# Constant matmuls in TensorE's planned gaps, and shorter matmul durations in the planner, in a two-layer decode kernel

## The chip, the cores and the metric

The kernel runs on one core of one Trainium2 chip. The metric is the device time of one execution in microseconds (us). The core has five engines with instruction streams of their own: TensorE (PE, matrix multiplies; its weight loads are shown as PEld), VectorE (DVE), ScalarE (ACT), GpSimd (POOL) and SyncE (SP), which here issues nearly all transfers from the chip's memory (HBM) to the core's on-chip memory. TensorE writes to PSUM, which has eight banks of 512 floats in each of 128 partitions; DVE and ACT read from there.

## The reference

Four sequences decode one token each (width 512) through two identical layers. One layer is a layer norm, attention with 32 query heads over 8 key/value heads (cache of 4096 positions, head size 128), a residual addition, a second layer norm, a gated feed-forward block of inner width 1792, and a residual addition.

```python
def _A_ref(x, k_cache, v_cache, wq, wo):
    q = (x @ wq).reshape(B, Sq, Hq, Dh) ...
    scores = jnp.einsum("bhqd,bhkd->bhqk", q, k) * (Dh ** -0.5)
    p = _softmax(scores, axis=-1)
    o = jnp.einsum("bhqk,bhkd->bhqd", p, v)
    return ... @ wo

def _B_ref(x, w_gate, w_up, w_down):
    g = jnp.einsum("bsd,df->bsf", x, w_gate)
    u = jnp.einsum("bsd,df->bsf", x, w_up)
    return jnp.einsum("bsf,fd->bsd", _sigmoid(g) * u, w_down)

x = A_x
x = x + _A_ref(_layernorm(x), A_k_cache, A_v_cache, A_wq, A_wo)
x = x + _B_ref(_layernorm(x), B_w_gate, B_w_up, B_w_down)
x = x + _A_ref(_layernorm(x), A_k_cache, A_v_cache, A_wq, A_wo)
x = x + _B_ref(_layernorm(x), B_w_gate, B_w_up, B_w_down)
```

Both layers use the same weights and the same caches.

## The kernel before

The attention work is cut into 16 units: sequence b (0 to 3), half of the key/value heads hg, layer l. Their order is written out in `seq`. A unit needs 8 tiles of keys and 8 of values, each 128 partitions by 2048 bf16 elements (512 KB). They land in a ring of 22 slots. The second layer's unit with hg 1 reuses the 8 key tiles and 6 of the 8 value tiles of the first layer's, which stay in their slots until then (`kept`); the other tiles are loaded again.

A unit runs like this. DVE transposes every key tile in place in 32x32 blocks (L575, 1.2 us each). TensorE multiplies the spread queries by the keys in two groups of 16 matmuls into S_ps (L582). DVE takes the maximum (L599) and a short chain makes the bias; ACT exponentiates (L615). The probabilities go through TensorE twice with an ACT copy after each (L622, L627, L633, L640) and come out transposed; L644 and L648 make the sum's reciprocal. TensorE multiplies them by the values in two groups of 64 matmuls into O_ps (L662); then a scaling copy (L668), a transposition (L672), a copy (L678), 64 matmuls with the output weights wo into M_ps (L684), and the residual addition (L699). After a sequence's second unit of a layer comes the feed-forward chain: layer norm (L710 to L730), gate and up (L760), tanh, product, five small matmuls (L782, L786), down (L796, 56 matmuls), addition (L804). After layer 0 it goes on to the next layer norm and the second queries (L535, 64 matmuls into Q_ps). `spread` (L555) lays the queries out through Q_ps and four ACT copies (L564) into qbd.

All of this is put in one list of operations, `S.put(engine, functions, reads, writes, cost, rank, ...)`. The planner `_Plan.schedule` (L102) plays the list with these costs in microseconds: each engine does one operation at a time, loads on "sp" go in their list's order at DMA_RATE megabytes per us, and of the operations that are ready the one with the lowest rank goes, or one that is ready soon (PATIENCE). What it fixes is the order of operations on each engine, which slot each tile gets, and with these the semaphore waits, which `emit` writes out. The costs themselves leave no trace in the program: nothing starts at a set time on the chip. A cost given for TensorE is multiplied by 0.75 (PACE).

Two PSUM banks, Q_ps and M_ps, are shared by many users one after another. A user that names `lock="Q"` or `"M"` holds the bank from its start until the operation with `free` of the same name has ended; the next holder waits for that one.

The ring's transfers are issued at L405, weights at L408, both on SyncE. A transfer into a used slot waits until the last reader of the tile in it is done.

Of the kernel before, what the change touches and what calls it, by code (L numbers as in the profile page):

```python
# [10 lines left out]
ENGINES = ("sp", "act", "pe", "dve", "pool")  # L11
LATENCY = 0.1
DMA_RATE = 0.42
DMA_DELAY = 1.6
PATIENCE = 2.0
PACE = {"pe": 0.75}

# [10 lines left out]
class _Op:  # L28
    def __init__(self, n, eng, fns, cost, rank, sem, inc):
        self.n = n  # L30
        self.eng = eng
        self.fns = fns
        self.cost = cost * PACE.get(eng, 1.0)
        self.rank = rank
        self.sem = sem
        self.inc = inc
        self.deps = set()
        self.order = set()
        self.lock = None
        self.free = None  # L40
        self.tile = None
        self.size = 0
        self.needed = inc == 16
        self.value = None
        self.start = None
        self.end = None


class _Plan:
# [3 lines left out]
    def __init__(self, slots):  # L53
        self.ops = []
        self.last_write = {}
        self.readers = {}
        self.slots = [None] * slots
        self.holder = {}

    def put(self, eng, fns, reads=(), writes=(), cost=0.1, rank=0.0, dma=None, size=0, lock=None, free=None, tiles=(), load=None):  # L60
# [41 lines left out]
    def schedule(self):  # L102
# [5 lines left out]
        bus = 0.0  # L108
        tenants = list(self.slots)
        locks = {}  # L110
        for op in self.ops:
# [33 lines left out]
        while done < len(self.ops):  # L145
            pick = None
            for e in ENGINES:
                if e == "sp":
                    if not loads or loads[0] not in ready:
                        continue  # L150
                    op = loads[0]
                    at = max(clock[e], ready[op])
                    if op.tile is not None:
# [3 lines left out]
                        at = max(at, s[0])  # L157
# [4 lines left out]
                for op in queue[e]:  # L162
                    at = max(clock[e], ready[op])
# [22 lines left out]
            at, op = pick  # L186
# [20 lines left out]
            if op.lock is not None:  # L207
                held = locks.get(op.lock)
                if held is not None:
                    self._after(op, held[1], True)  # L210
                locks[op.lock] = (None, None)
            if op.free is not None:
                locks[op.free] = (op.end + LATENCY, op)
            done += 1
            for u in users.get(op, ()):
                left[u] -= 1
                if not left[u]:
                    arrive(u)
        self.span = max(op.end for op in self.ops)
        self.prog = {e: sorted((o for o in self.ops if o.eng == e), key=lambda o: (o.start, o.n)) for e in ENGINES}  # L220
# [4 lines left out]
        for e in ENGINES:  # L225
            for op in self.prog[e]:
                if op.needed:
                    count[op.sem] = count.get(op.sem, 0) + op.inc
                    op.value = count[op.sem]

    def emit(self, eng, e, sems):
# [15 lines left out]
def bass_interleave_layers__gqa_block_cached__glu_gated_glu__decode_kernel(nc, A_x, A_k, A_v, A_wq, A_wo, B_x, B_wg, B_wu, B_wd, out):  # L247
# [85 lines left out]
    def bank(name, new=False):  # L333
        tenure[name] += new
        return f"{name}t{tenure[name]}"
# [113 lines left out]
    for i in range(1, len(seq) + 1):  # L449
# [15 lines left out]
        "pe", lambda e: e.matmul(M_ps[:, 0:4], lhsT=ones[:], rhs=xsum[:, 0:4], start=True, stop=True),  # L465
        reads=["xsum1", "ones"], writes=["M0"], cost=0.4,
    )
# [38 lines left out]
    def first_q(hg):  # L506
        fns = []
        for s in range(NS):
            g = hg * NS + s
            for h in range(R):  # L510
                for k in range(KD):
                    c0 = (g % 2 * R + h) * DH
                    fns.append(lambda e, s=s, g=g, h=h, k=k, c0=c0: e.matmul(
                        Q_ps[:, (s * R + h) * B:(s * R + h + 1) * B], lhsT=wq[:, g // 2, k, c0:c0 + DH], rhs=xT[:, :, k],
                        start=(k == 0), stop=(k == KD - 1),
                    ))
        r = 0.0 if hg == 0 else 0.6
        S.put("pe", fns, reads=["xT", f"wq{2 * hg}", f"wq{2 * hg + 1}"], writes=[bank("Q", True)], cost=2.1, rank=r, lock="Q")
        S.put(
            "act",  # L520
            lambda e: e.activation(
                q1[:, hg * NS:(hg + 1) * NS].rearrange("p g h b -> p (g h b)"), Q_ps[:, 0:64], ACTF.Copy
            ),
            reads=[bank("Q")], writes=[f"q1{hg}"], cost=0.25, rank=r, free="Q",
        )

    def second_q(b, hg, rank):
        fns = []
        for s in range(NS):
            g = hg * NS + s  # L530
            for h in range(R):
                for k in range(KD):
                    c0 = (g % 2 * R + h) * DH
                    c = s * R + h
                    fns.append(lambda e, g=g, k=k, c0=c0, c=c: e.matmul(  # L535
                        Q_ps[:, c:c + 1], lhsT=wq[:, g // 2, k, c0:c0 + DH], rhs=xT[:, b, k:k + 1],
                        start=(k == 0), stop=(k == KD - 1),
                    ))
        S.put("pe", fns, reads=[f"xT{b}", f"wq{2 * hg}", f"wq{2 * hg + 1}"], writes=[bank("Q", True)], cost=2.1, rank=rank, lock="Q")
        S.put(  # L540
            "act", lambda e: e.activation(q2[:, hg, :], Q_ps[:, 0:16], ACTF.Copy),
            reads=[bank("Q")], writes=[f"q2{hg}"], cost=0.2, rank=rank, free="Q",
        )

    def spread(i, rank):
# [7 lines left out]
        for n in range(NQ):  # L553
            for a in range(4):
# [3 lines left out]
                ))  # L558
        S.put("pe", fns, reads=[key, "ident"], writes=[bank("Q", True)], cost=0.5, rank=rank, lock="Q")
        fns = []  # L560
# [6 lines left out]
    def unit_scores(i):  # L567
        b, hg, l = seq[i]
        qi, rank = i % 2, float(i)
        for q in range(2):  # L570
# [9 lines left out]
            for nn in range(NQ):  # L580
                for s, t in enumerate(ts):
# [5 lines left out]
                    ))  # L587
            S.put("pe", fns, reads=[f"qbd{qi}"], writes=[f"S{q}"], tiles=ts, cost=1.85, rank=rank)

    def unit_probs(i):  # L590
# [30 lines left out]
        for c in range(8):  # L621
            fns.append(lambda e, c=c: e.matmul(  # L622
                PT_ps[:, c * 64:(c + 1) * 64], lhsT=p_sb[:, c, :], rhs=sel_p[:], start=True, stop=True,
            ))
        S.put("pe", fns, reads=["p_sb", "sel_p"], writes=["PT"], cost=0.65, rank=rank)
        S.put(
# [4 lines left out]
        for t4 in range(4):  # L631
            for a in range(4):
# [3 lines left out]
                ))  # L636
        S.put("pe", fns, reads=["pt1", "ident"], writes=["PT"], cost=0.65, rank=rank)
        pt = pt_sb[i % 2]
# [13 lines left out]
    def unit_values(i):  # L652
# [3 lines left out]
        for q in range(2):  # L656
            ts = [tile("v", b, hg, l, s, q) for s in range(NS)]
            fns = []
            for tt in range(TH):
                t = q * TH + tt  # L660
                for s, v in enumerate(ts):
# [3 lines left out]
                    ))  # L665
            S.put("pe", fns, reads=[f"pt_sb{i % 2}"], writes=["O"], tiles=ts, cost=1.75, rank=rank)
        S.put(
# [14 lines left out]
        for n in range(16):  # L682
# [9 lines left out]
            "pe", fns, reads=[f"oT{b}{hg}", f"wo{2 * hg}", f"wo{2 * hg + 1}"], writes=[bank("M", True), f"own{b % 2}" if first else f"own_{b}"],  # L692
            cost=1.8, rank=rank, lock="M",
        )
# [55 lines left out]
    def glu(b, l, rank):  # L750
# [14 lines left out]

        S.put("pe", wide(wg, G_ps), reads=[f"xT{b}", "wg"], writes=["G"], cost=1.55, rank=rank)
        rstd(b, 4.0, rsh[:, c:c + 1], f"rsh{c}", rank)
        S.put("pe", wide(wu, U_ps), reads=[f"xT{b}", "wu"], writes=["U"], cost=1.55, rank=rank)
        S.put(
# [24 lines left out]
        for i, (a, w) in enumerate(parts):  # L794
            for j in range(4):
# [3 lines left out]
                ))  # L799
        S.put("pe", fns, reads=["hT", "wd", "wd_r0", "wd_r1"], writes=["U"], cost=1.5, rank=rank)  # L800
        o = xin[:, b, :] if last else x[:]
# [49 lines left out]
    S.put("pool", lambda e: None, reads=outs)  # L851

    S.schedule()
    with nc.Block() as block:
# [37 lines left out]
```

## Time and profile before

| what | value |
|---|---|
| time, median of 3 runs | 359.93 us (357.55 to 362.03) |
| the profiled execution: its time, its span | 356.54 us, 354.1 us |
| mean granted TensorE clock in the profile | 0.805 |
| PE, PEld busy | 208.1 us (59%), 145.4 us (41%), 5,724 instructions each |
| DVE, ACT busy | 171.6 us (48%), 80.1 us (23%) |
| HBM read | 118.76 MB, 335 GB/s over the span |
| score matmuls L582 | 512, busy 49.0 us |
| value matmuls L662 | 2,048, busy 51.7 us |
| output projection L684 | 1,024, busy 22.1 us |
| key transpositions L575 (DVE) | 96, busy 114.6 us |
| instructions in all | 12,495 |

The span is the time from the first to the last instruction in one profiled execution; 2.4 us lie around it. The page's second part cuts the span into 40 slices of 8.9 us; a digit is the busy share in tenths, PEclk the clock granted to TensorE in tenths of full speed, GB/s what the transfers moved. The chain of waits follows the work back from the last instruction, at each step to what released it; "issue" is time in which an engine waited for nothing that the profile shows. In the timeline a row is a run of equal instructions: start, duration, engine, line, operation, output and inputs, count, and in brackets the idle time before it and what ended that. In the view by windows the columns are the window, its length, the busy time of PE, PEld, DVE, ACT and POOL with their instruction counts, the granted clock, the busy share of the DMA engines and GB/s.

### The profile page before, as it was taken

The page shows a single profiled execution, that of the slowest core. Times are in us where ns is not written, and L with a number is a line of the kernel's source. Part 1 is how long each engine was busy: PE and PEld are TensorE (multiplying, and loading weights), DVE is VectorE, ACT ScalarE, POOL GpSimd, SP SyncE. Part 2 cuts the span into 40 slices and gives each one's busy share as a digit, 9 for nine tenths or more (in the row PEclk, how much of TensorE's full clock was granted, in tenths as well). Part 3 has the DMA queues.
Part 4 walks back from the last instruction along what each step waited for, and adds up shares of the span by engine and source line. Part 5 has one row for each costly group of instructions (what it writes and reads, how often), then busy time and mean ns, then how long its engine had stood idle before and what let it go on. Part 6 is the DMA issues. An engine that isn't in the chain of part 4 may idle for free.

```text
span 354.1 us, 12495 instructions
## 1 busy us (share of the span) xinstructions
PE 208.1 (59%) x5724; PEld 145.4 (41%) x5724; DVE 171.6 (48%) x303; ACT 80.1 (23%) x231; POOL 12.9 (4%) x35
## 2 busy tenths in 40 slices
PE   0345423257585727787756368859645586767564
PEld 0315202142354615465435153636343545464352
DVE  4770760047305728605827567237458475247301
ACT  0413001001222211424113211533030313322021
POOL 6100000000000000100000000000000000000000
PEclk9999999999758667956888768685868558758889
DMA  7999999999989998889999996889999959899200
GB/s 277 385 401 408 409 351 381 411 409 403 344 320 329 412 407 325 281 303 382 410 408 409 406 381 222 274 292 413 409 406 409 408 207 325 279 409 405 89 4 2
DMA packets 37060, 119.57 MB, mean 338 GB/s; under 512 B 3472, under 2 KB 7824, under 8 KB 37008
## 3 DMA queue, kind: packets, MB, share of 16 engines
q1 hardware_dynamic: 36944, 118.76, 88.7%
q8 instruction: 45, 0.74, 0.8%
q14 instruction: 7, 0.06, 0.0%
q10 hardware_dynamic: 64, 0.01, 0.0%
HBM read 118.76 MB, written 0.00 MB: 335 GB/s over the span
## 4 chain that ended last, share of the span: by engine, by line
PE 38%; DMA 23%; SPq 12%; issue 12%; DVE 8%; ACT 6%; ACTq 0%; DVEq 0%
DMA ring<-in_A_k_cache_dram 10%; DMA ring<-in_A_v_cache_dram 9%; PE O_ps L662 9%; PE S_ps L582 8%; SPq L405 8%; PE M_ps L684 5%; SPq L408 4%; DVE ring L575 4%; DMA wd_r<-in_B_w_down_dram 4%; PE Q_ps L535 3%; PE G_ps L760 2%; ACT p_sb L615 2%; PE U_ps L796 2%; PE U_ps L760 2%; PE PT_ps L622 1%
## 5 line engine op out<-in xcount | busy, mean ns | idle before, releaser
L575 DVE STREAM_TRANSPOSE ring<-ring 128x1024 int32<-128x1024 int32 x96 | 114.6, 1224 | 39.9 <-DMA ring<-in_A_k_cache_dram 39.4
L662 PE MATMUL O_ps<-ring,pt_sb 128*4 128x128 bf16 x2048 | 51.7, 282 | 33.7 <-DMA ring<-in_A_v_cache_dram 19.3
L582 PE MATMUL S_ps<-ring,qbd 128*16 128x512 bf16 x512 | 49.0, 511 | 23.5 <-DVE ring L575 19.2
L662 PEld LDWEIGHTS O_ps<-ring,pt_sb 128*4 128x4 bf16 x2048 | 46.0, 112 | 40.1 <-issue 31.3
L599 DVE TENSOR_REDUCE ml<-S_ps 128x1 f32<-128x1024 f32 x16 | 19.6, 1223 | 54.0 <-PE S_ps L582 54.0
L615 ACT ACTIVATE p_sb<-S_ps,stat 128x1024 bf16<-128x1024 f32 x16 | 19.3, 1204 | 51.0 <-DVE stat L612 50.9
L582 PEld LDWEIGHTS S_ps<-ring,qbd 128*16 128x16 bf16 x512 | 13.1, 103 | 43.1 <-DVE ring L575 19.7
L684 PE MATMUL M_ps<-wo,oT 128*1 128x128 bf16 x1024 | 22.1, 251 | 7.8 <-issue 6.0
L668 ACT ACTIVATE o_sb<-O_ps,stat 128x128 bf16<-128x128 f32 x16 | 5.9, 368 | 82.8 <-PE O_ps L662 79.0
L684 PEld LDWEIGHTS M_ps<-wo,oT 128*1 128x1 bf16 x1024 | 18.9, 98 | 11.6 <-issue 7.8
L622 PE MATMUL PT_ps<-sel_p,p_sb 128*128 128x64 bf16 x128 | 8.9, 229 | 21.6 <-ACT p_sb L615 21.6
L564 ACT ACTIVATE qbd<-Q_ps 32x64 bf16<-32x64 f32 x64 | 13.7, 214 | 28.3 <-PE Q_ps L555 27.4
L535 PE MATMUL Q_ps<-xT,wq 128*128 128x1 bf16 x512 | 14.8, 164 | 8.3 <-issue 7.8
L746 POOL TENSOR_TENSOR stat<-stat 128x1 f32<-128x1 f32 x12 | 6.5, 542 | 326.3 <-DVE stat L742 282.1
L535 PEld LDWEIGHTS Q_ps<-xT,wq 128*128 128x128 bf16 x512 | 14.3, 100 | 9.0 <-issue 8.1
L622 PEld LDWEIGHTS PT_ps<-sel_p,p_sb 128*128 128x128 bf16 x128 | 6.6, 119 | 24.8 <-ACT p_sb L615 24.3
L648 DVE RECIPROCAL stat<-M_ps 128x1 f32<-128x1 f32 x16 | 2.7, 167 | 28.6 <-PE M_ps L644 28.5
L640 ACT ACTIVATE pt_sb<-PT_ps 128x512 bf16<-128x512 f32 x16 | 9.5, 597 | 14.8 <-PE PT_ps L633 14.7
L627 ACT ACTIVATE pt<-PT_ps 128x512 bf16<-128x512 f32 x16 | 9.6, 597 | 11.3 <-PE PT_ps L622 10.8
L699 DVE SCALAR_TENSOR_TENSOR xs<-M_ps,xs 128x128 f32<-128x128 f32 x12 | 3.5, 289 | 17.8 <-PE M_ps L684 17.8
L633 PE MATMUL PT_ps<-pt,ident 128*32 128x128 bf16 x256 | 9.7, 294 | 3.9 <-ACT pt L627 3.6
L796 PE MATMUL U_ps<-wd,hT 128*1 128x128 bf16 x384 | 7.6, 230 | 7.2 <-DMA wd_r<-in_B_w_down_dram 3.4
(89 smaller groups left out, 187.7 us busy)
## 6 DMA issues: line engine op xcount, KB each, us to landing
ring<-in_A_v_cache_dram SPq DMA_DIRECT2D x104, 512.0 KB, 12.1
ring<-in_A_k_cache_dram SPq DMA_DIRECT2D x96, 512.0 KB, 10.9
wq<-in_A_wq_dram SPq DMA_DIRECT2D x4, 1024.0 KB, 11.9
wo<-in_A_wo_dram SPq DMA_DIRECT2D x4, 1024.0 KB, 15.0
wg<-in_B_w_gate_dram SPq DMA_DIRECT2D x1, 1792.0 KB, 13.6
wu<-in_B_w_up_dram SPq DMA_DIRECT2D x1, 1792.0 KB, 16.9
wd<-in_B_w_down_dram SPq DMA_DIRECT2D x1, 1536.0 KB, 21.2
wd_r<-in_B_w_down_dram SPq DMA_DIRECT2D x2, 128.0 KB, 16.0
```

The costliest lines, as they stand in the source:

```text
L405: S.put("sp", lambda e: e.dma_start(ring[t.slot], src), dma="ring", load=t, size=0.524, cost=0.45)
L408: S.put("sp", lambda e: e.dma_start(o, i), writes=[key], dma=key, size=size, cost=0.45)
L535: fns.append(lambda e, g=g, k=k, c0=c0, c=c: e.matmul(Q_ps[:, c:c + 1], lhsT=wq[:, g // 2, k, c0:c0 + DH], rhs=xT[:, b, k:k + 1], start=(k ...
L575: "dve", lambda e, t=t: e.transpose(ring[t.slot].bitcast(dt.int32), ring[t.slot].bitcast(dt.int32)),
L582: fns.append(lambda e, s=s, t=t, nn=nn, q=q: e.matmul(S_ps[32 * s:32 * s + 16, q * 512:(q + 1) * 512], lhsT=qbd[:, qi, s, nn, :], rhs=ring ...
L599: dve(lambda e: e.tensor_reduce(ml[:, 0:1], S_ps[:], AX.X, ALU.max, negate=True), ["S0", "S1"], ["ml"], 1.22)
L615: lambda e: e.activation(p_sb[:].rearrange("p c x -> p (c x)"), S_ps[:], ACTF.Exp, bias=nbias, scale=rs, accum_out=ls),
L622: fns.append(lambda e, c=c: e.matmul(PT_ps[:, c * 64:(c + 1) * 64], lhsT=p_sb[:, c, :], rhs=sel_p[:], start=True, stop=True,))
L662: fns.append(lambda e, s=s, v=v, t=t, tt=tt: e.matmul(O_ps[32 * s:32 * s + R, 0:DH], lhsT=pt[:, t % 4, t // 4, s, :], rhs=ring[v.slot][:, ...
L684: fns.append(lambda e, n=n, j=j: e.matmul(M_ps[32 * j:32 * j + 1, P:2 * P], lhsT=oT[:, b, hg * 16 + n:hg * 16 + n + 1], rhs=wo[:, hg * 16 ...
L760: fns.append(lambda e, k=k, j=j: e.matmul(o_ps[32 * j:32 * j + 1, 0:FS], lhsT=xT[:, b, k:k + 1], rhs=w[:, k, j * FS:(j + 1) * FS], start=( ...
L796: fns.append(lambda e, i=i, a=a, w=w, j=j: e.matmul(U_ps[32 * j:32 * j + 1, 0:P], lhsT=a, rhs=w[:, j * P:(j + 1) * P], start=(i == 0), sto ...
```

## The change

Two things are done. First, the planner's numbers are new: PACE is gone, the costs of the TensorE operations are set one by one, and four constants of the planner change. Where a cost is not named in the diff, the planner now takes the full number in place of 0.75 of it.

```diff
-LATENCY = 0.1
-DMA_RATE = 0.42
+LATENCY = 0.06
+DMA_RATE = 0.41
 DMA_DELAY = 1.6
-PATIENCE = 2.0
-PACE = {"pe": 0.75}
+PATIENCE = 1.0
+FILL = 0.75
+FILL_US = 0.105
...
-        self.cost = cost * PACE.get(eng, 1.0)
+        self.cost = cost
```

| TensorE operation | planned before (cost x 0.75) | planned after |
|---|---|---|
| queries, 64 matmuls (L513, L535) | 1.58 | 1.8 |
| spread (L555) | 0.38 | 0.3 |
| score group (L582) | 1.39 | 1.05 |
| probabilities (L622, L633) | 0.49 | 0.42 |
| value group (L662) | 1.31 | 1.08 |
| output projection (L684) | 1.35 | 1.1 |
| gate, up (L760) | 1.16 | 0.95 |
| down (L796) | 1.13 | 0.98 |

Second, when the plan is complete, a new step looks at each pair of neighbours in TensorE's planned order. Where the planned gap between them has room, it puts in one operation of n filler matmuls, n being 0.75 of the gap divided by 0.105 us, rounded down. It takes the bank Q, or else M, if the plan has no holder of it during the fillers' planned time and some holder has released it before. The operation waits for that last release (an ACT or DVE operation) and for two constants. It signals nobody and stands in TensorE's stream between the two neighbours.

```diff
+    def fill(self, held_by):
+        pe = sorted((o for o in self.ops if o.eng == "pe"), key=lambda o: (o.start, o.n))
+        for a, b in zip(pe, pe[1:]):
+            at, room = a.start + a.cost, (b.start - a.start - a.cost) * FILL
+            n = int(room / FILL_US)
+            if n < 1:
+                continue
+            for name, fn in self.fillers:
+                until = at + n * FILL_US
+                held = held_by.get(name, [])
+                if any(x[0] < until and (x[1] is None or x[1] > at) for x in held):
+                    continue
+                last = [x for x in held if x[1] is not None and x[1] <= at]
+                if not last:
+                    continue
+                op = _Op(len(self.ops), "pe", [fn] * n, n * FILL_US, 99.0, "pe", 1)
+                op.start, op.end = at, until
+                op.deps.add(last[-1][2])
+                for k in self.filler_reads:
+                    op.deps.add(self.last_write[k])
+                self.ops.append(op)
+                break
...
+    for name, ps_ in (("Q", Q_ps), ("M", M_ps)):
+        S.fillers.append((name, lambda e, ps_=ps_: e.matmul(
+            ps_[:, 264:512], lhsT=ident[:], rhs=hsum[:].bitcast(bf)[:, 0:248], start=True, stop=True,
+        )))
+    S.filler_reads = ["ident", "hsum"]
     S.schedule()
```

A filler multiplies the constant `ident` (128x128 bf16) by 248 columns of the constant `hsum` and writes 248 columns of the bank that nothing reads. The times at which a bank is held (`held_by`) are noted by the planner as it goes; the very first matmul into M_ps (L465) now takes the lock of M, so that M counts as held from there on. The list of transfers and all computed values stay as they were.

## The prediction

> **What bounds the kernel now.** The page comes first: the slices and the queues.
>
> ```profile
> PE   0345423257585727787756368859645586767564
> PEclk9999999999758667956888768685868558758889
> GB/s 277 385 401 408 409 351 381 411 409 403 344 320 329 412 407 325 281 303 382 410 408 409 406 381 222 274 292 413 409 406 409 408 207 325 279 409 405 89 4 2
> q1 hardware_dynamic: 36944, 118.76, 88.7%
> q8 instruction: 45, 0.74, 0.8%
> ```
>
> The core moves 118.76 MB and the best slices reach about 410 GB/s: 290 us is the floor of the transfers, and the last 24 us (from 330) have none. The transfers end near 328 us, so some 35 us of transfer time are lost in dips, near 100, 145, 215 and 290 us. The transfer queue's own waits name who makes the dips:
>
> ```profile
> SPq L405 <- PE O_ps L662: 76.0, 11, 11.9
> ```
>
> The ring slot of the next tile is freed by the matmuls that read the last tile in it. The chain of waits agrees:
>
> ```profile
> PE 38%; DMA 23%; SPq 12%; issue 12%; DVE 8%; ACT 6%; ACTq 0%; DVEq 0%
> ```
>
> TensorE with its "issue" is half the span. Then I asked for the clock by window (columns: PE and weight-load busy, ..., clock, DMA share, GB/s) and for TensorE's timeline:
>
> ```profile
> 140.90:147.70 6.80, 5.11 (x134) 2.84 (x131) 5.93 (x13) 2.23 (x9) 0.54 (x1) 1.00 0.80 267
> 154.60:161.40 6.80, 5.85 (x165) 4.01 (x157) 0.26 (x1) 0.42 (x2) 0.00 (x0) 0.50 0.80 260
> 175.00:178.40 3.40, 0.00 (x0) 0.00 (x0) 1.89 (x2) 0.00 (x0) 0.00 (x0) 1.00 1.02 404
> 178.40:181.80 3.40, 3.29 (x52) 1.66 (x56) 0.00 (x0) 0.55 (x2) 0.00 (x0) 0.51 1.04 413
> 182.00:185.20 3.20, 1.79 (x92) 1.29 (x84) 2.32 (x7) 0.22 (x2) 0.00 (x0) 1.00 1.02 405
> ```
>
> ```profile
> 47.89 1.89 PE L582 MATMUL S_ps<-ring,qbd 128*16 128x512 bf16 x16 [3.24 <-DVE ring L575]
> 139.87 1.04 PE L582 MATMUL S_ps<-ring,qbd 128*16 128x512 bf16 x16
> 159.17 1.92 PE L582 MATMUL S_ps<-ring,qbd 128*16 128x512 bf16 x16
> ```
>
> Two clocks are granted, 1.00 and 0.50, and the same 16 score matmuls take 1.04 or 1.9 us. After 3.4 us without a matmul (175.0 to 178.4) the clock is half; after 3.4 us with 3.29 us of them it is full again. At 47.89 they took 1.89 us too, though the page shows 9 there: until about 90 us the clock row is not to be believed, and the array ran at half. The last thing to see is what "issue" is:
>
> ```profile
> 238.82 0.94 PE L535 MATMUL Q_ps<-xT,wq 128*128 128x1 bf16 x30 [3.84 <-issue]
> ...
> 252.26 0.56 PE L662 MATMUL O_ps<-ring,pt_sb 128*4 128x128 bf16 x27 [3.53 <-issue]
> 252.61 1.20 PE L582 MATMUL S_ps<-ring,qbd 128*16 128x512 bf16 x16
> 253.74 0.29 PE L672 MATMUL M_ps<-ident,o_sb 128*128 128x128 bf16 x1
> 253.96 1.88 PE L582 MATMUL S_ps<-ring,qbd 128*16 128x512 bf16 x16
> 255.63 1.70 PE L684 MATMUL M_ps<-wo,oT 128*1 128x128 bf16 x64
> 257.16 0.18 PE L555 MATMUL Q_ps<-q,ident 128*32 128x16 bf16 x4
> 258.56 0.24 PE L555 MATMUL Q_ps<-q,ident 128*32 128x16 bf16 x12 [1.22 <-issue]
> ```
>
> TensorE stops in the midst of a group. From one stop to the next it ran 27+16+1+16+64+4 = 128 matmuls, with their weight loads 256 instructions; q8's packets are 0.74 MB / 45 = 16.4 KB each, 64 bytes for each of 256. These stops wait for program text, and from 252.26 to 258.56 a block of 256 needed 6.3 us. The view of waits has 15 such stops on TensorE, 34 us in all, 14 of them after 90 us.
>
> **The change, part by part.**
>
> *Clock.* What the half clock costs, by line, is busy time less the number of groups by the time of a group at full clock (1.04 scores, 1.04 values, 1.06 wo, 0.79 gate/up, 0.97 down, 0.42 for each half of the probabilities' transposition): L582 49.0-32x1.04 = 16; L662 51.7-32x1.04 = 18; L684 22.1-16x1.06 = 5; L760 21.7-16x0.79 = 9; L796 10.2-8x0.97 = 2; L622 and L633 18.6-32x0.42 = 5. Sum 55 of 173 us; query projections take 1.6 to 1.8 us per 64 at either clock and gain nothing. Some 13 us of it lie before 90 us, beside transfers at 400 GB/s, and are worth nothing there: 42 are left. Of these lines the chain holds about 29% of the span (8.9 values, 8.2 scores, 4.6 wo, some 7 the rest), 103 us, 97 of them after 90 us; at 42/143 excess that is 28 us on the path, all of it only if the fillers hold the clock at full, as 75% filled gaps should by the windows above. Now the fetch: 11,448 matmuls and loads are 45 blocks, 38 of them after 90 us, and 14 of the 38 already end in a stop. There the block's arrival, not the clock, ends the work: a faster burst only makes the stop longer. 28x(1-14/38) = 18; a block or two falls under 6 us by the gain itself: 17. Ends: 0 (every block becomes late) and 28.
>
> [...]
>
> *Fillers, number.* TensorE is busy 36 us of the first 90 and 172 of the 264 after. At full clock the latter would be 130. The planner knows no stops; if its plan of this part lasts between 224 us (the 290 us floor and the tail of 24, less 90) and 264, its gaps are 95 to 134 us, 3/4 of it 71 to 100, at 0.105 us 680 to 950 fillers; gaps under 0.14 us get none, others round down. I take 550 after 90 us and 400 before it: 1,900 instructions, 7 blocks.
>
> *Fillers, price of one.* 248 columns: four L760 matmuls run side by side, so 16 of 448 columns in 0.79 us are 0.44 ns a column, 0.109 us. The weight load before it is at most 29 ns in a stream (34 pairs of L535 in 1.00 us): 0.109 to 0.138, so 78 to 99% of the gap in place of 75%, and no overrun while the clock is full. At half clock it is 0.22: 1.5 gaps. [...]
>
> *Fillers, instructions.* 550 after 90 us are 1,100 instructions, 4.3 blocks; at most 4.3x6.3 = 27 us, at least 0, for a run of 128 fillers lasts 13 us, twice a fetch, and cannot starve by itself. [...] I take 5, near the lower end.
>
> *The added wait.* A filler waits for the last release of its bank (an ACT or DVE copy), and the next real TensorE work queues behind it. Nearest rows: S_ps after the qbd copy 1.7 us in 3, M_ps L684 after oT 1.6 in 6. Between 0 and 4 us, taken 0: Q is released twice or so per unit, long before most gaps.
>
> *Order.* Latency, patience, rate and durations change the plan's order on all engines but not the list of transfers on SyncE; a ring slot may change. The one visibly misplaced wait is 3.4 us (down projection on wd_r). Between -5 and +5, taken 0. The lock on the first M_ps matmul moves nothing: no other M work is ready then.
>
> Sum: 354.1-17+5 = 342, and with the 2.4 us outside the span 344.5 against the profiled 356.54. The median of the runs is 1.0095 times that run: 348 us, 3.3% under 359.93.
>
> **The rivals.** (1) *The fetch eats the gain* (24%). More work at full clock, but each block still arrives every 6.1 to 6.3 us under transfers; stops grow from 34 to 50 us. For it: the 38 blocks after 90 us already average 6.9 us. Against: long tracts without a stop, as 128 to 157 us. Within 6 us of the old: 354 to 366. (2) *TensorE becomes fetch-bound by the fillers* (17%), the slower side. If the 4.3 blocks fall into tracts where fetches are back to back (163 to 201, 249 to 262, 305 to 329 us), they cost 27 us against the 17; with stops that throw the clock back (175 to 178) a third of the gain goes as well: 354.1+27-11 = 370 span, 376 in terms of the median. It decides as soon as over 17/6.3 = 2.7 blocks, 345 fillers, are paid in full. (3) *The clock does not stay up* (5%): stops and small gaps leave windows too empty, fillers run at 0.22 us and overrun by half of 95 us of gaps, at worst +47, with half of it hidden +24: 382. (4) *Larger gain* (part of the forecast's side): all 28 us on the path and dips closed: 330.
>
> **Chances.** Forecast, 54%, 332 to 352. A measurement of this kernel tells about 2% (7 us) from no change. Faster 0.54, same 0.24, slower 0.22. Leaving out some 5% below and 12% above: 332 to 370.
>
> **What would show it.** Clock windows at 1.00 in most of 100 to 330 us, and from about 20 us on score groups of 1.04 in place of 1.89; L582 near 35 us, L662 near 36. About 950 more matmuls on a new line and 52 packets in q8. Dips of the slices shallower, the last transfer at 317 in place of 328. "Issue" at 12 to 14% of the chain. Wrong, if the new matmuls' line stands on the chain with more than 10 us, if "issue" passes 60 us, or if score groups after 100 us still average 1.5.

## The result, and the profile after

The changed kernel takes 373.55 us (median, 371.97 to 375.48) where the kernel before takes 360.98 beside it: 1.038 of it, with a 95% interval of 1.028 to 1.048. The forecast was 348; the ratio makes it slower by 14 us. Executions of one kernel are sorted into fast and slow ones (of the kernel before, beside e1, 357.6 to 362.9 us and 364.4 to 367.4 us): the ratios here compare fast ones, the medians are of all, and the profiles of e1, e7 and e15 below are of slow ones. The page's lines that answer to those shown of before:

```profile
PE   0498979688877789965769889949687989877886
PEclk9999999699556599996878999965869999865999
GB/s 277 408 397 409 397 348 399 410 408 367 389 284 347 412 360 123 235 368 397 409 407 408 408 149 119 368 394 403 409 407 408 312 115 166 358 359 410 201 2 4
q8 instruction: 52, 0.85, 0.9%
...
PE 41%; DMA 18%; issue 13%; SPq 12%; DVE 11%; ACT 5%; ACTq 0%; DVEq 0%
DMA ring<-in_A_v_cache_dram 10%; PE O_ps L695 8%; SPq L438 8%; DVE ring L608 6%; PE S_ps L615 6%; PE M_ps L717 6%; PE Q_ps L887 4%; DMA ring<-in_A_k_cache_dram 4%; DMA wd_r<-in_B_w_down_dram 4%; SPq L441 4%; PE M_ps L887 3%; PE G_ps L793 2%; PE U_ps L793 2%; PE Q_ps L568 2%; ACT p_sb L648 2%
```

TensorE is busy nearly everywhere (78% of the span, 59% before), and its clock is at 9 in 15 of the last 30 slices, where before had 2. Yet the dips of the transfers are deeper: 123, 149 and 119, 115 GB/s where before had 281 to 325, 222 and 207. Slices are 9.2 us here, so the last transfer ends near 346 us, 17 us later than before. (Lines are numbered anew: L615 scores, L695 values, L717 output projection, L732 residual addition, L608 key transposition, L887 fillers.) The fillers' lines hold 7% of the chain, 27 us, over the 10 that the prediction named as a sign of being wrong. And DVE, which was 8% of the chain, has 11.

Two groups of TensorE's instructions, after:

```profile
L887 PE MATMUL Q_ps<-hsum,ident 128*128 128x248 bf16 x726 | 97.0, 281 | 1.1 <-issue 1.1
L615 PE MATMUL S_ps<-ring,qbd 128*16 128x512 bf16 x512 | 39.9, 431 | 9.8 <-DVE ring L608 6.7 <-issue 2.6 <-ACT qbd L597 0.3
```

The windows after 90 us (stretch, its length, then busy time of each engine with its number of instructions, TensorE first; the granted clock, the DMA share and GB/s last), after and then before:

```profile
90.00:369.70 279.70, 223.32 (x5473) 156.07 (x5473) 128.39 (x238) 64.67 (x188) 6.03 (x11) 0.83 0.80 304
```

```profile
90.00:354.10 264.10, 171.89 (x4953) 122.84 (x4953) 130.06 (x241) 65.73 (x188) 5.96 (x11) 0.74 0.86 322
```

The fillers raise the clock: after 90 us it goes from 0.74 to 0.83, and the scores' busy time falls from 49.0 to 39.9 us. So far the forecast holds. What it doesn't have is in DVE's waits, before and after:

```profile
DVE xs L699 <- PE M_ps L684: 20.6, 11, 6.8
```

```profile
DVE xs L732 <- PE M_ps L717: 59.5, 16, 8.3
```

DVE stands three times as long before residual additions, waiting for the output projection. DVE's timeline shows what is queued behind, at the same place of the program; before, and then after:

```profile
115.97 6.86 DVE L575 STREAM_TRANSPOSE ring<-ring 128x1024 int32<-128x1024 int32 x6
124.00 0.29 DVE L699 SCALAR_TENSOR_TENSOR xs<-M_ps,xs 128x128 f32<-128x128 f32 x1 [1.17 <-PE M_ps L684]
128.03 1.22 DVE L599 TENSOR_REDUCE ml<-S_ps 128x1 f32<-128x1024 f32 x1 [3.74 <-PE S_ps L582]
```

```profile
119.21 3.48 DVE L608 STREAM_TRANSPOSE ring<-ring 128x1024 int32<-128x1024 int32 x3
128.59 0.29 DVE L732 SCALAR_TENSOR_TENSOR xs<-M_ps,xs 128x128 f32<-128x128 f32 x1 [5.90 <-PE M_ps L717]
128.79 3.49 DVE L608 STREAM_TRANSPOSE ring<-ring 128x1024 int32<-128x1024 int32 x3
133.50 1.22 DVE L632 TENSOR_REDUCE ml<-S_ps 128x1 f32<-128x1024 f32 x1 [1.22 <-PE S_ps L615]
```

Before, DVE did all six key transpositions while TensorE worked, then the addition. After, the plan puts the addition behind three of them; on the chip DVE waits 5.9 us for it, and the other three, which run the moment it is over, stand in line. The maximum of the scores starts at 133.50 in place of 128.03. How much of that the line on DVE makes, this view does not say: fillers stand before the scores too (e13).

I call this the standing: DVE's idle time right before a residual addition whose next instruction is a key transposition that starts at once, summed over the timeline (the additions after the feed-forward part count too, idle times under 0.3 us do not). It is 8.2 us before and 55.7 after.

### The profile page after: what moved, and what is told of

Same layout as the page of the kernel before. It is cut to its first block, busy times and chain, and to the rows that moved or that the text cites. A ratio compares the mean times of both kernels' runs of the same rounds, so it can differ in the third digit from the quotient of the medians.

```text
span 369.7 us, 14222 instructions
## 1 busy us (share of the span) xinstructions
PE 288.3 (78%) x6588; PEld 205.9 (56%) x6588; DVE 170.7 (46%) x303; ACT 79.3 (21%) x231; POOL 13.1 (4%) x35
## 4 chain that ended last, share of the span: by engine, by line
PE 41%; DMA 18%; issue 13%; SPq 12%; DVE 11%; ACT 5%; ACTq 0%; DVEq 0%
DMA ring<-in_A_v_cache_dram 10%; PE O_ps L695 8%; SPq L438 8%; DVE ring L608 6%; PE S_ps L615 6%; PE M_ps L717 6%; PE Q_ps L887 4%; DMA ring<-in_A_k_cache_dram 4%; DMA wd_r<-in_B_w_down_dram 4%; SPq L441 4%; PE M_ps L887 3%; PE G_ps L793 2%; PE U_ps L793 2%; PE Q_ps L568 2%; ACT p_sb L648 2%
## 5 line engine op out<-in xcount | busy, mean ns | idle before, releaser
L608 DVE STREAM_TRANSPOSE ring<-ring 128x1024 int32<-128x1024 int32 x96 | 114.4, 1223 | 33.4 <-DMA ring<-in_A_k_cache_dram 33.0
L887 PE MATMUL Q_ps<-hsum,ident 128*128 128x248 bf16 x726 | 97.0, 281 | 1.1 <-issue 1.1
L887 PEld LDWEIGHTS Q_ps<-hsum,ident 128*128 128x128 bf16 x726 | 68.6, 103 | 19.8 <-issue 10.0
L695 PE MATMUL O_ps<-ring,pt_sb 128*4 128x128 bf16 x2048 | 40.8, 241 | 16.9 <-issue 8.9
L695 PEld LDWEIGHTS O_ps<-ring,pt_sb 128*4 128x4 bf16 x2048 | 34.8, 94 | 24.1 <-issue 20.5
L615 PE MATMUL S_ps<-ring,qbd 128*16 128x512 bf16 x512 | 39.9, 431 | 9.8 <-DVE ring L608 6.7
L717 PE MATMUL M_ps<-wo,oT 128*1 128x128 bf16 x1024 | 22.6, 245 | 18.8 <-issue 17.8
L717 PEld LDWEIGHTS M_ps<-wo,oT 128*1 128x1 bf16 x1024 | 17.8, 94 | 24.1 <-issue 19.6
L615 PEld LDWEIGHTS S_ps<-ring,qbd 128*16 128x16 bf16 x512 | 11.2, 92 | 26.5 <-issue 13.4
L732 DVE SCALAR_TENSOR_TENSOR xs<-M_ps,xs 128x128 f32<-128x128 f32 x12 | 3.5, 292 | 47.1 <-PE M_ps L717 47.1
L887 PE MATMUL M_ps<-hsum,ident 128*128 128x248 bf16 x138 | 22.2, 318 | 0.0
L597 ACT ACTIVATE qbd<-Q_ps 32x64 bf16<-32x64 f32 x64 | 13.6, 213 | 25.0 <-PE Q_ps L588 24.4
L887 PEld LDWEIGHTS M_ps<-hsum,ident 128*128 128x128 bf16 x138 | 14.8, 114 | 3.3
## 6 DMA issues: line engine op xcount, KB each, us to landing
wg<-in_B_w_gate_dram SPq DMA_DIRECT2D x1, 1792.0 KB, 13.6
wd_r<-in_B_w_down_dram SPq DMA_DIRECT2D x2, 128.0 KB, 16.3
```

The costliest lines, as they stand in the source:

```text
L597: fns.append(lambda e, o=o, v=v: e.activation(o, v, ACTF.Copy))
L608: "dve", lambda e, t=t: e.transpose(ring[t.slot].bitcast(dt.int32), ring[t.slot].bitcast(dt.int32)),
L615: fns.append(lambda e, s=s, t=t, nn=nn, q=q: e.matmul(S_ps[32 * s:32 * s + 16, q * 512:(q + 1) * 512], lhsT=qbd[:, qi, s, nn, :], rhs=ring ...
L695: fns.append(lambda e, s=s, v=v, t=t, tt=tt: e.matmul(O_ps[32 * s:32 * s + R, 0:DH], lhsT=pt[:, t % 4, t // 4, s, :], rhs=ring[v.slot][:, ...
L717: fns.append(lambda e, n=n, j=j: e.matmul(M_ps[32 * j:32 * j + 1, P:2 * P], lhsT=oT[:, b, hg * 16 + n:hg * 16 + n + 1], rhs=wo[:, hg * 16 ...
L887: S.fillers.append((name, lambda e, ps_=ps_: e.matmul(ps_[:, 264:512], lhsT=ident[:], rhs=hsum[:].bitcast(bf)[:, 0:248], start=True, stop= ...
```

## The experiments

Times are medians; ratios are to the kernel before in the same batch. A difference of ratios is turned into time with 360 us; by the two intervals together it is uncertain by 3 to 6 us. "Theory" is the name that the expectations give to a possible cause; they say what each would make of the time.

| kernel | us | ratio, 95% interval | standing, us |
|---|---|---|---|
| the change | 373.6 | 1.038 (1.028 to 1.048) | 55.7 |
| e1 change, no fillers | 379.6 | 1.049 (1.039 to 1.059) | 58.3 |
| e3 change, fillers of 8 columns | 387.3 | 1.078 (1.070 to 1.086) | 61.0 |
| e4 change, early fillers only | 384.3 | 1.072 (1.065 to 1.079) | 57.9 |
| e2 old plan, fillers | 364.8 | 1.012 (1.007 to 1.017) | 18.0 |
| e8 old plan, wide fillers | 356.9 | 0.997 (0.991 to 1.003) | 18.4 |
| e6 durations only, no fillers | 370.1 | 1.035 (1.020 to 1.049) | 31.2 |
| e7 constants only, no fillers | 362.8 | 1.011 (1.005 to 1.017) | 23.3 |
| e5 change, projection planned late | 362.4 | 1.013 (0.999 to 1.027) | 0.0 |
| e12 e5 without fillers | 366.7 | 1.016 (1.001 to 1.031) | 0.0 |
| e10 e5 with wide fillers | 357.6 | 0.993 (0.988 to 0.998) | 0.0 |
| e9 change, addition's rank raised | 374.8 | 1.039 (1.022 to 1.056) | 1.7 |
| e14 e1, only DVE's order altered | 368.6 | 1.026 (1.016 to 1.037) | 4.5 |
| e13 change, only DVE's order altered | 371.9 | 1.036 (1.025 to 1.047) | 3.8 |
| e15 before, only DVE's order altered | 380.6 | 1.060 (1.049 to 1.070) | 65.9 |
| e17 e13 with wide fillers | 371.0 | 1.036 (1.019 to 1.054) | 3.7 |
| e18 e13 with fewer fillers | 368.8 | 1.033 (1.018 to 1.049) | 6.7 |
| e16 before, projection planned at 2.5 | 359.8 | 1.008 (1.002 to 1.014) | 4.6 |
| e11 e16 with wide fillers | 353.5 | 0.980 (0.967 to 0.994) | 3.4 |

**The change without its fillers (e1).**

```diff
-        self.fill(held_by)
```

> The changed kernel without its fillers: the new durations, the new order and the new ring slots stay. Theory F (instructions): the fillers' program text is what costs, so without its 7 blocks the time falls to the old one or below, 350 to 361 us, with stops for program text at about 40 us of the chain. Theory O (occupancy): the fillers stand on TensorE ahead of real work, 27 us on the chain after the change; without them 350 to 361 as well, but see the narrow fillers. Theory P (plan): the new order alone makes the deep dips of the transfers (110 to 150 GB/s near 145, 225 and 300 us); then the time stays at 368 or more and the same dips show. The clock falls back to about 0.8 in the record in each case.

Theory P holds: without fillers the kernel is no faster but if anything slower, 1.049. The new plan alone costs (1.049-1)x360 = 17.6 us, and the fillers give some 4 back. The plan lowers the clock a little as well: over the whole run 0.75 and 0.77 are granted in the runs compared, 0.78 to 0.83 in those of the kernel before beside them.

**Narrow fillers (e3).**

```diff
-            ps_[:, 264:512], lhsT=ident[:], rhs=hsum[:].bitcast(bf)[:, 0:248], start=True, stop=True,
+            ps_[:, 264:272], lhsT=ident[:], rhs=hsum[:].bitcast(bf)[:, 0:8], start=True, stop=True,
```

> The changed kernel with fillers of 8 columns in place of 248: as many instructions, but about 0.03 us each in place of 0.11, 25 us of TensorE in place of 95. Theory F: as slow as the change, 370 to 376, since the blocks of program text are the same. Theory O: near the kernel without fillers, within 3 us. Theory P: equal to the kernel without fillers, and both at 368 or more. If the clock is what the fillers give, it is about 0.8 here as without them.

No theory had 387. It splits the fillers into their two halves. The group of this kernel's Q fillers, and then its window after 90 us:

```profile
L887 PE MATMUL Q_ps<-hsum,ident 128*128 128x8 bf16 x726 | 32.7, 169 | 2.6 <-issue 2.6
```

```profile
90.00:385.90 295.90, 207.94 (x5486) 146.64 (x5478) 130.41 (x244) 64.97 (x189) 6.02 (x11) 0.66 0.76 288
```

They take 33 us of TensorE where those of 248 columns took 97, and the clock is 0.66 after 90 us. Over the whole run it is 0.74 to 0.76, no more than e1 has without fillers. What is left of them is their program text and these 33 us (39 with bank M's), and it costs (1.078-1.049)x360 = 10.4 us, 0.012 us for a pair of instructions. That it is mostly the text is argued from the stops: TensorE's matmuls stand for "issue" for 39.8 us in e3, and for 29.9 in e1 and 21.8 in e14, which have no fillers. Making them 248 columns wide wins (1.078-1.038)x360 = 14.4 us back: that is the clock, from 0.66 to 0.83, net of the time that they take.

**Early fillers only (e4).**

```diff
-            if n < 1:
+            if n < 1 or at > 95.0:
```

> The changed kernel with fillers only before 95 us of planned time, where the transfers run at 400 GB/s anyway. Theories F and O: the early fillers cost nothing on the path, time as without fillers, within 3 us, 350 to 361. Theory P: as without fillers, 368 or more.

A miss of every theory: 1.072, (1.072-1.049)x360 = 8 us over the kernel without fillers, though the transfers bound that stretch (384 GB/s up to 90 us, at a DMA share of 1.01). The third maximum of the scores starts at 87.0 us here and at 88.0 in the kernel before, so nothing is lost up to there. The reason stays open; the standing is that of e1. The same run also prices the other 496 fillers: the change has them on top of these 368 and is (1.072-1.038)x360 = 12 us faster.

**The old plan with fillers (e2).**

```diff
-LATENCY = 0.06
-DMA_RATE = 0.41
+LATENCY = 0.1
+DMA_RATE = 0.42
...
-PATIENCE = 1.0
+PATIENCE = 2.0
+PACE = {"pe": 0.75}
```

(and the old costs)

> The old constants and durations, hence the old order and slots, with the fillers put into the old plan's gaps at the same 0.75 and 0.105 us. Theories F and O: slower than before, 366 or more. Theory P: the fillers give their gain on the old order, 345 to 356, with score groups of 1.04 us in most of the run.

Between the theories: 1.012. On the old plan 715 fillers cost 4 us, far less than the new plan with or without them. But they bring no gain either, although the clock goes up:

```profile
90.00:360.20 270.20, 207.05 (x5360) 147.52 (x5358) 129.12 (x238) 65.85 (x188) 5.95 (x11) 0.84 0.84 315
```

The clock goes from 0.74 to 0.84 and the scores' busy time from 49.0 to 41.1 us, but TensorE's stops for "issue" grow from 33.7 to 48.7 us, and the standing grows from 8.2 to 18.0. This is the prediction's rival (1) nearly to the number: stops of 50 us, and a time of 354 to 366.

**Durations alone, constants alone (e6, e7).** The kernels are the old one with only one half of the planner's numbers new, without fillers.

> The old constants, the new durations, no fillers. Theory D: the durations are what moves the addition forward (planned after 5 and 3 transpositions in place of 8 and 5): most of the 20 us of the kernel without fillers, 370 or more. If patience, latency and rate carry it: 362 or less.

> The new constants (latency, rate, patience), the old durations, no fillers. Theory D: the planned addition is still behind 8 transpositions in the first of the two places and behind 3 in place of 5 in the second: between, 360 to 370. If the constants carry the loss: 375 or more.

The shorter durations carry most of the plan's loss (1.035), the three constants (latency, rate, patience) a smaller part (1.011); 0.035+0.011 = 0.046 is near the 0.049 of both together.

**The output projection planned late (e5), and without fillers (e12).**

```diff
-            cost=1.1, rank=rank, lock="M",
+            cost=4.0, rank=rank, lock="M",
```

> The changed kernel with one planned duration altered: the output projection 4.0 us in place of 1.1, so that the plan puts DVE's residual addition behind the ready key transpositions (8 and 7 of them, as before the change) and not after 3. 659 fillers are left of 864. Theory D (DVE stands in line): the shorter durations let the plan place the addition early on DVE's in-order stream; on the chip it waits there 59.5 us for the output projection, 20.6 before, with ready transpositions behind it. By it the wait falls to 35 us or less and the time to 366 or less. Theory S (slots and the order on TensorE): the addition's place is a by-product; the time stays above 370. By the plan's own span, 334 against 316, it should be 18 us slower: 392.

> The late output projection without fillers. The same change of plan took 11 us off with fillers. By theory D it takes as much or more off without: 379.6 falls to 362 to 369, so that the fillers are worth 0 to 6 us here as well. If it lands under 361, the fillers are a loss on a good plan.

One planned duration that is further from the truth (the group takes 1.06 us without a stop) takes 9 us off with fillers and 12 without. But the wait that I had named did not fall:

```profile
DVE xs L732 <- PE M_ps L717: 61.8, 11, 10.8
```

The sum of the waits was the wrong measure. No ready transposition is behind the additions any more: the standing is 0.0. From here on the standing is what I go by. But the altered duration may move the order on every engine, so this run by itself does not show that the standing made the difference.

**The addition moved by its rank (e9).**

```diff
-            cost=0.4, rank=rank, free="M",
+            cost=0.4, rank=rank + 1.5, free="M",
```

> The changed kernel, all planned durations as in the change, but the residual addition's rank raised by 1.5, so that the plan puts it behind the key transpositions of the next unit; 949 fillers. Idle of DVE before a residual addition that has a key transposition right behind it was 8.2 us before the change, 55.7 after, 58.3 without fillers, 31.2 with the durations alone, 23.3 with the constants alone and 0.0 with the late output projection. Theory D, now by this sum: near 0 here too, and 358 to 368. Theory S (the late output projection helped by TensorE's order): 370 or more.

A miss for theory D as it stood: the standing is 1.7 us and the time is still 374.8. The chain of waits of this kernel by engine and line:

```profile
PE 53%; DMA 17%; issue 12%; DVE 8%; ACT 8%; ACTq 0%; SPq 0%; DVEq 0%
PE Q_ps L887 11%; PE O_ps L695 10%; PE S_ps L615 9%; DMA ring<-in_A_k_cache_dram 8%; DMA ring<-in_A_v_cache_dram 8%; PE M_ps L717 5%; ACT p_sb L648 3%; PE Q_ps L568 2%; DVE ml L632 2%; PE U_ps L829 2%; PE G_ps L793 2%; DMA xin<-in_A_x_dram 2%; PE PT_ps L655 1%; PE U_ps L793 1%; PE M_ps L887 1%
```

The rank moves additions that a layer norm waits for as well, the planner makes new gaps of that and puts 949 fillers there, and these are now 12% of the chain, 45 us. So this run changed three things at once and tells little.

**DVE's order alone, both ways (e14, e13, e15).** Here the plan is made first, and then only DVE's stream is rearranged. In e13 and e14 up to three key transpositions that follow an addition within 6 us of the plan go ahead of it, unless a maximum (cost 1.22) comes between:

```diff
+    def late_adds(self, most=3, within=6.0):
+        dve = sorted((o for o in self.ops if o.eng == "dve"), key=lambda o: (o.start, o.n))
+        for i, op in enumerate(dve):
+            if not op.add:
+                continue
+            at, n = op.start, 0
+            for nxt in dve[i + 1:]:
+                if nxt.cost == 1.22 or n == most or nxt.start > at + within:
+                    break
+                if nxt.key:
+                    n += 1
+                    nxt.start = at - 0.01 * (most + 1 - n)
```

In e15, the kernel before, each addition goes ahead of up to three transpositions right before it (`op.start = prv.start - 0.01`).

> The same move on DVE in the changed kernel without fillers (379.6). The four kernels without fillers so far lose 0.4 us of time for each us that DVE stands so (8 us: 359.5; 23: 362.8; 31: 370.1; 58: 379.6). Theory D: the standing falls below 25 us and the time to 362 to 370. Theory S: 376 or more.

> The kernel before, with only one thing altered after the planning: on DVE each residual addition is put ahead of up to three key transpositions that stand right before it. No fillers, old order elsewhere. Theory D: the loss can be made at will, 366 to 376 in place of 360. Theory S: within 3 us of 360.

Both go the way theory D has it; e15's loss, 21 us, is larger than its 6 to 16. The same place of the program in e14, DVE's timeline:

```profile
118.35 4.93 DVE L622 STREAM_TRANSPOSE ring<-ring 128x1024 int32<-128x1024 int32 x4
125.24 0.29 DVE L747 SCALAR_TENSOR_TENSOR xs<-M_ps,xs 128x128 f32<-128x128 f32 x1 [1.96 <-PE M_ps L732]
128.24 1.23 DVE L647 TENSOR_REDUCE ml<-S_ps 128x1 f32<-128x1024 f32 x1 [2.71 <-PE S_ps L630]
```

No transposition is left behind the addition, and the maximum starts at 128.24, as early as before the change. In e15 the standing is made at will, DVE and then TensorE:

```profile
124.77 0.29 DVE L712 SCALAR_TENSOR_TENSOR xs<-M_ps,xs 128x128 f32<-128x128 f32 x1 [6.15 <-PE M_ps L697]
124.98 3.49 DVE L587 STREAM_TRANSPOSE ring<-ring 128x1024 int32<-128x1024 int32 x3
```

```profile
128.52 1.89 PE L595 MATMUL S_ps<-ring,qbd 128*16 128x512 bf16 x16 [3.87 <-DVE ring L587]
```

TensorE waits for the transpositions that waited for the addition that waited for TensorE. This alone takes the old kernel from 360 to 381 us, 1.060. In e14 its removal gives (1.049-1.026)x360 = 8 us (3 to 13 by the intervals) of the plan's 17.6; the other 9 are not found. They may lie in TensorE's order or the ring slots. The standing does not set the time alone: e14 with 4.5 us of it is at 1.026, e16 below with 4.6 at 1.008.

> The changed kernel, with its fillers, slots and the orders on TensorE, ACT and SyncE as planned; only on DVE, after the planning, up to three key transpositions that follow a residual addition within 6 us are pulled ahead of it. Theory D: DVE no longer stands before the addition with ready transpositions behind it; 357 to 367 in place of 373.6. Theory S (TensorE's order and the slots carry the plan's loss): within 3 us of 373.6.

Theory S by its number: with the fillers the repair gives no measurable gain (1.038 to 1.036). So in the change itself the standing is not shown to cost anything. The same place of the program shows why it can be so; DVE and then TensorE:

```profile
118.07 4.60 DVE L623 STREAM_TRANSPOSE ring<-ring 128x1024 int32<-128x1024 int32 x4
128.18 0.29 DVE L748 SCALAR_TENSOR_TENSOR xs<-M_ps,xs 128x128 f32<-128x128 f32 x1 [5.50 <-PE M_ps L733]
133.09 1.23 DVE L648 TENSOR_REDUCE ml<-S_ps 128x1 f32<-128x1024 f32 x1 [4.62 <-PE S_ps L631]
```

```profile
127.85 1.85 PE L631 MATMUL S_ps<-ring,qbd 128*16 128x512 bf16 x16
129.62 2.40 PE L904 MATMUL Q_ps<-hsum,ident 128*128 128x248 bf16 x21
131.95 1.10 PE L631 MATMUL S_ps<-ring,qbd 128*16 128x512 bf16 x16
```

The transpositions are done by 122.7 us and none waits behind the addition, yet the maximum starts at 133.09 where the change has 133.50. Between the two groups of scores stand 21 fillers, 2.4 us: they fill the gap in which TensorE waits 2.2 us for DVE's transpositions in e1, without fillers, and they stay there when DVE no longer makes it wait. The chain of e13:

```profile
PE 46%; DMA 22%; DVE 13%; issue 9%; ACT 5%; SPq 3%; ACTq 0%; DVEq 0%
DMA ring<-in_A_k_cache_dram 17%; PE S_ps L631 9%; PE Q_ps L904 8%; DVE ring L623 7%; PE O_ps L711 7%; PE M_ps L733 4%; DMA ring<-in_A_v_cache_dram 3%; PE M_ps L904 3%; SPq L453 3%; ACT p_sb L664 2%; PE Q_ps L583 2%; DVE ml L648 2%; PE G_ps L810 2%; PE U_ps L810 2%; PE PT_ps L671 2%
```

The fillers (L904) went from 7 to 11% of the chain. What DVE no longer holds up, they do: that is shown at the place above and argued for the rest. Two more runs were to tell whether it is their text or their time.

> The change with the key transpositions pulled ahead (371.9), its fillers replaced by 354 of 448 columns in bank Q, for 864 of 248: as long on TensorE, 510 pairs of instructions fewer. With fillers that kernel stops 39 us for program text, without them 22. Theory F (instructions): 0.009 us a pair, 4.6 us less, 365 to 369. Theory O (the fillers' time in front of real work): 370 to 374.

> The same kernel with the fillers of the change, but 0.4 of each planned gap in place of 0.75: 422 for 864, about half the time on TensorE and half the instructions. Theory F: 4 us less by the instructions, and some of the clock lost: 366 to 371. Theory O: the overruns go, 360 to 366.

Neither is settled: 371.0 and 368.8, with intervals that hold both answers and e13 too. In e17 TensorE's stops for "issue" fall from 39.1 to 28.8 us, and no gain of time is seen.

**Wide fillers (e8, e10, e11) and the plan of the fastest kernel (e16).** A wide filler takes 448 columns of wq in place of 248 of hsum and writes bank Q alone; half as many are needed.

```diff
-FILL_US = 0.105
+FILL_US = 0.197
...
-            ps_[:, 264:512], lhsT=ident[:], rhs=hsum[:].bitcast(bf)[:, 0:248], start=True, stop=True,
+            ps_[:, 64:512], lhsT=ident[:], rhs=wq[:, 0, 0, 0:448], start=True, stop=True,
```

> The old plan with fillers of 448 columns in bank Q alone, 329 in place of 715: 1.3 blocks of program text fewer after 90 us, for nearly the same busy time. The narrow fillers cost 7.7 us for 864, so 0.009 us each. Theory F: 3 us less than the old plan with the fillers of the change (364.8): 359 to 363. If the fillers' time on TensorE is what costs, 365 or more.

> The late output projection with 257 fillers of 448 columns in bank Q alone in place of 659. At 0.009 us each: 3.5 us less than 362.4, so 357 to 361; if the clock suffers from the missing fillers (bank M is not used): 362 or more.

> The old plan with 303 wide fillers and the output projection planned at 2.5 us in place of 1.35. The old plan with wide fillers has 18.4 us of the idle that theory D names. By theory D that falls and the time with it: 348 to 354; else 355 to 360.

> The kernel before with the output projection planned at 2.5 us in place of 1.35, no fillers: the plan of the fastest kernel so far (353.5 with 303 wide fillers) by itself. If the wide fillers make that kernel's gain: 357 to 362. If the order makes it: 351 to 355.

On the old plan 386 pairs fewer give (1.012-0.997)x360 = 5 us, 0.014 us a pair; e10 against e5, 402 pairs fewer, 7 us. The stops for "issue" fall by as much, from 48.7 to 38.3 us and from 34.6 to 28.2. Within the uncertainty both agree with the price from the narrow fillers on the new plan; on the plan of e17 it is not seen. But the wide fillers also hold TensorE for less time (81 us in e8, 101 in e2) and leave bank M alone, and no run separates these from the text. The last two separate order from fillers: the late projection alone gives nothing (1.008), wide fillers on that plan (1.008-0.980)x360 = 10 us, where on the old plan they give 1; why they pay so differently is open. That kernel, e11, beats both the kernel before and the change, 0.980 with an interval of 0.967 to 0.994 from three runs. Its clock and dips:

```profile
PEclk9996999789858698985859899785876999665999
GB/s 274 381 401 407 408 357 374 410 409 402 335 362 352 412 407 374 263 258 366 403 409 408 407 403 271 335 241 411 406 409 409 408 301 262 285 393 407 191 4 2
```

The dips are 241 to 263 GB/s where before has 207 to 281, and they are no longer than before. The windows of the same kernel, after 90 us:

```profile
90.00:348.80 258.80, 199.51 (x5122) 127.69 (x5120) 129.74 (x241) 65.48 (x188) 5.97 (x11) 0.82 0.88 329
```

With 303 fillers its clock there is 0.82, where the change has 0.83 with 864.

## Why the prediction was wrong, step by step

**The step that failed is *Order***: "Between -5 and +5, taken 0", because "The one visibly misplaced wait is 3.4 us". It was +17.6 us (e1, 14 to 21). I looked for waits that the new plan might remove, and not for those that a plan can make. The planner's durations had been longer; that slack kept the residual additions behind the transpositions on DVE (the shorter durations alone, e6, raise the standing from 8 to 31 us). With the short durations the plan takes TensorE to be done early, and DVE, which runs its instructions in the plan's order, then stands where the plan has no wait. Without fillers DVE's order alone carries 8 of the 17.6 us in the new plan, and it makes 21 in the old one; 9 stay open. With the fillers in, the same repair gave nothing measurable (e13), so what holds the change back place by place is only in part known. None of my rivals had it: the slower one was about program text. Its mechanism was there, but at 10.4 us for all 864 fillers and not 27 for those after 90 us.

**A second term was put at nothing: the fillers before 90 us.** The prediction counts 400 of them, worth nothing there, and prices instructions only for the 550 later ones. The 368 that e4 keeps cost 8 us, for a reason that is open. The 496 later ones then take 12 us off (e4 to the change), which is the -17+5 that the forecast has for them. That agreement holds on this plan only. All fillers together give 4 us on the new plan, cost 4 on the old one (e2) and give 1 with the late projection (e12 to e5), against the 12 of the forecast; on the old plan rival (1) came true.

**Clock.** Right in mechanism: 17 us forecast, 14.4 net of the fillers' own time (e3 to the change). That the sizes are near is in part luck: the forecast starts from a clock of 0.74 and this pair from 0.66, and on the old plan no net gain is left (e2). Only 0.83 was reached, and scores and values came to 39.9 and 40.8 us where I expected 35 and 36. The rows from which I took that gaps filled to 75% hold the clock up did not show it: one window with 5.11 of 6.80 us busy was at 1.00, another with 5.85 at 0.50. In the change TensorE is busy for 80% of the time after 90 us, and the clock is 0.83.

**Instructions.** Right in kind, low in size: 5 us forecast for the 550 after 90 us, 10.4 measured for all 864, 0.012 us a pair. That it would be near the lower end of 0 to 27 us was an estimate of mine that no run shows. The stops of TensorE's matmuls grew from 34 to 39 us in the change, and to 49 in e2. A stop in the midst of the output projection, and the price of fillers, at half clock and at full:

```profile
105.13 1.63 PE L887 MATMUL M_ps<-hsum,ident 128*128 128x248 bf16 x7
...
133.38 3.35 PE L887 MATMUL Q_ps<-hsum,ident 128*128 128x248 bf16 x30
...
166.19 0.51 PE L717 MATMUL M_ps<-wo,oT 128*1 128x128 bf16 x24 [0.27 <-ACT oT L711]
170.46 1.24 PE L717 MATMUL M_ps<-wo,oT 128*1 128x128 bf16 x40 [3.76 <-issue]
```

**Fillers' number and price.** 864 in place of 950, 520 of them after 90 us in place of 550 (5,473 matmuls for 4,953). The second hit is in part luck: the prediction's sum gives 680 to 950 there, and 550 was taken without a worked step. One takes 0.112 us at full clock (30 in 3.35) and 0.23 at half, as worked out. The run of 30 above has a load before each matmul; the 30 loads, 95 ns or more each, start with the matmuls at 133.38 and take 3.08 us, within the matmuls' 3.35: in this run the loads are hidden.

The text comes in 52 packets now, as forecast: 0.85 MB / 52 = 16.3 KB each, where before had 16.4, and 2x6,588 = 13,176 matmuls and loads are 51.5 blocks of 256.

**The sum.** Forecast -17+5+0 = -12; measured -14.4+10.4+17.6 = +13.6 us on 360, which is 1.038. That these three close is no proof, since they are the steps of one path, from before to e1, to e3 and to the change; what bears on the parts by themselves are e14 and e15 for the order and, less cleanly, the wide fillers for the text. By way of e4 the same 13.7 us are 17.6 for the order, 8.3 for the early fillers and -12.2 for the later ones. (Two figures of the prediction were off by its own rows: in rival (3) 354.1+24+2.4, times 1.0095, is 384 and not 382, and from 290 to 328 us 38 us of transfer time are lost in dips, not 35.)

## What to carry to other kernels

A planner's costs are also its margins: here, shortening them to durations measured at full clock made the program slower (1.035 in e6), because an engine that works in a fixed order was told to wait for work that came late for reasons that the plan doesn't know. Before a planner is retuned, list for each in-order engine the operations that wait for another engine, and ask what ready work would be queued behind them if that engine came 5 us late; keep such work ahead. Fillers for the clock have a price of their own, here, it seems, mostly in program text: on two plans fewer and longer ones did better (by 5 us in e8, 7 in e10), on a third no difference was seen (e17). Test filler and plan apart, and fillers by the stretch that they stand in: the early ones here only cost (8 us in e4).

## What was not expected of the hardware

Even tiny instructions have a price: 864 pairs that hold TensorE for some 39 us in all cost 10.4 us of time, and TensorE's stops are 39.8 us with them, 22 to 30 without fillers. Narrow fillers don't raise the clock: 0.74 to 0.76 over the whole run, 0.75 and 0.77 without fillers, 0.86 to 0.88 with those of 248 columns. And fillers in a stretch that the transfers bound (384 GB/s up to 90 us) cost 8 us (e4), for which these runs have no explanation.
